# Block attention into a mixture of experts: another order of first loads and constants, later value sums, and routing in three batches

## The chip, the cores and the metric

One core of one Trainium2 chip runs the kernel. The metric is the device time of one execution in microseconds (us). The engines are PE (TensorE), DVE (VectorE), ACT (ScalarE), POOL (GpSimd) and SP (SyncE, which here issues DMAs); PEld is the weight load of PE.

## The reference, cut to what matters

First the attention, for 4 batches, 8 heads, 768 positions and 64 columns. Each query sees the keys within 15 positions on either side, and one summary of each of the 24 blocks of 32 keys: the maximum of the keys and the mean of the values. Then a mixture of experts on the 3072 rows of 512 columns that come out: 4 groups of 4 experts, of which each row goes to one.

```
k_sum = k.reshape(B, H, nb, block, D).max(axis=3)
v_sum = v.reshape(B, H, nb, block, D).mean(axis=3)
mask_l = np.abs(pos[:, None] - pos[None, :]) < window
scores_s = scale * np.einsum('bhsd,bhnd->bhsn', q, k_sum) + np.log(block)
scores_all = np.concatenate([np.where(mask_l, scores_l, -1e9), scores_s], axis=-1)
a = softmax(scores_all)
x = np.matmul(a, np.concatenate([v, v_sum], axis=2))   # then as (3072, 512)
g_idx = argmax(x @ w_group);  e_idx = argmax(x @ w_expert[g_idx])
w = softmax(group logits)[g_idx] * softmax(expert logits)[e_idx]
out[tok] = w * (relu(x[tok] @ w1[g, e]) @ w2[g, e])    # w1 512x1024, w2 1024x512
```

## The kernel before

**Attention.** The work goes by pairs of heads: `idx` = 0 to 15, and each pair has three steps of four tiles of 64 queries, so a step is `n` = 3 idx + g, from 0 to 47. `PLAN` (L46) sets what a step does and in which order: scores of step n (`scores`, L724: PE into `ps_s`, DVE's `ss` with the row maximum `nm`, then ACT's `pr` in `exps`), the transposes of the step before (`transpose_p`), the products with the values of the step before that (`values`), and pieces of the preparation of the next pair (`prep`, L685). Of a pair, `load_qk` (L559) loads `qn` and `kn` (128x768 each), `repack` (L668) copies them into `qr` and `kr`, `prep` transposes them on PE into `ktp` and `qbd`, reduces the key maxima `ks` and builds `kw`. `load_vw` (L573) loads the value windows `va` of a pair, in four DMAs (two of 96x10x64 and two of 80x2x64), into a ring of four; `init_va` (L612) sets the parts that no DMA writes. `load_vn` (L586) loads the values of four heads, 96x2048; `v_summaries` (L645) halves them on POOL five times, and a sixth operation makes the means `vs`. `put_vs` (L655) moves the means of a pair to the right partitions by two DMAs (`vr`), which SP issues, and POOL spreads `vr` over `va` with `pool_copy` (L1211, a multiplication by one). The table `VN` (L55) says at which pair a batch's half is loaded (third number) and summed (fourth).

**Order.** The program runs each engine's instructions in the order in which the code issues them; nothing is reordered. An engine waits at an instruction until its inputs are there, and everything behind it waits too. The DMAs that SP issues are such a row as well. Before the loop stands the start-up sequence (L814 to L833).

**Routing.** `Router.consts` (L164) makes constants by IOTA on POOL, some of which DVE finishes (`lower`, `ones`, `seen`). `Router.route` (L227) takes a batch of columns of 128 tokens (24 in all): maxima, one-hot rows (`goh`, `eoh`), then `ranks` (L265) with matmuls of `eb` by `tri` and `ones`, from which come each token's place and its one-hot row `ohr`, and the weights `w_all`. It is a generator that the attention's loop and later the experts' loop drive a step at a time, through a first-in, first-out list `work`. The first 12 columns are routed from step 28 on, then `first_blocks` picks the rows of the first four experts' blocks; the last 12 (`fin`, L1251) run after the attention. `slots` (L372) makes the table of the tokens of a block: it compares (`eq`), multiplies with three columns, the token number on POOL and the two halves of the weight on DVE (`bo`), and multiplies on PE with `ohr`. From the result come `gather`, `weight` and `scatter`. `unit_slots` (L503) does so for the units, whose columns it takes from three look-ups.

**Experts.** `Experts` (L895) multiplies in two parts: ACT casts a weight to `w1h` or `w2h`, and a subtraction gives the rest, `w1l` or `w2l` (`split_w`, L969); the activations are split alike (`hTh`, `hTl`, `xT`). `first` (L1136) works the first four blocks, `rest` (L1159) the pairs of units. `hook` (L1221) places the first weights' loads, gathers and splits at steps near the end of the attention; `W1_COPY` and `W1_POOL` move parts of the split of w1 to POOL. `gather` (L983) reads rows of x by an indirect DMA from POOL; `y` is the product of an output with its weight.

Of the kernel before, what the change touches and what calls it, by code (L numbers as in the profile page):

```python
# [20 lines left out]
P = 128  # L21
# [42 lines left out]
SPLIT_AT = (-4, -3, 1, 2)  # L64
W1_COPY, W1_POOL = (0,), (0, 1)
# [70 lines left out]
class Router:  # L136
# [235 lines left out]
    def slots(self, name, col, nt, step, c0):  # L372
# [4 lines left out]
        for j0 in range(0, nt, step):  # L377
            js = slice(j0, j0 + step)
            bo = self.tmp.tile([P, step, 3, n], F32R, name="bo_" + name, bufs=2)
            eq = self.tmp.tile([P, step, n], F32, name="eq_" + name, bufs=2)  # L380
            V.tensor_tensor(out=eq, in0=iob.broadcast_to([P, step, n]), in1=bc(col[:, js], n), op=ALU.is_equal)
            yield
            nc.gpsimd.tensor_tensor(out=bo[:, :, 0], in0=eq, in1=bc(self.tok1[:, js], n), op=ALU.mult)
            for i in range(2):
                V.tensor_tensor(out=bo[:, :, 1 + i], in0=eq, in1=bc(self.w[:, js, i].bitcast(F32), n), op=ALU.mult)
                yield
            yield from self.pause(SLOT_AHEAD)
            if j0 == 0:
                sl = self.ps["tr" if nt == step else "lg"].next()[:, 0:3 * n].rearrange("p (a s) -> p a s", a=3)
            for j in range(step):  # L390
                jj = j0 + j
                self.T.matmul(out=sl.rearrange("p a s -> p (a s)"), lhsT=self.ohr[:, jj],
                                 rhs=bo[:, j].rearrange("p a s -> p (a s)"), start=(jj == 0), stop=(jj == nt - 1))
# [127 lines left out]
def attention(tc, q, k, v, w_group, w_expert, ident, pool_copy, x_dram, ps, router, hook):  # L521
# [24 lines left out]
    with ExitStack() as st, ExitStack() as nat_st:  # L546
# [284 lines left out]
        for t in prr:  # L831
            V.memset(t[:, :, NC:NR], 1.0)
# [469 lines left out]
```

## Time and profile before

| what | before |
|---|---|
| time, median of 3 runs | 594.27 us (593.92 to 594.61) |
| time of the profiled execution | 593.2 us |
| its span, first to last instruction | 591.5 us |
| mean granted clock of PE | 0.951 of full |
| busy PE, DVE, ACT, POOL | 527.7, 361.9, 289.3, 207.7 us |
| PE busy share in 40 slices, tenths | 5369899898989796897999999999999999999992 |
| DMA busy share in 40 slices, tenths | 9939699998634452049965566667765665538600 |

A slice is 14.8 us. PE is busy 89% of the span; its low digits stand in the first three slices, in the 16th and 17th (222 to 251 us) and in the last. The time beside the span (593.2 less 591.5) is 1.7 us.

### The profile page before, as it was taken

Reading aid. Unit: us, or ns where it says so; the run is one execution under the profiler, and the core shown is the slowest. Engines: PE = TensorE matmul, PEld = TensorE weight load, DVE = VectorE, ACT = ScalarE, POOL = GpSimd, SP = SyncE. Lnnn points to the kernel's source line nnn. Section 1 sums busy time; section 2 is a strip of 40 time slices with the busy share of each in tenths; the row PEclk is TensorE's granted clock in tenths of the full one; section 3 lists DMA queues with packets and bytes.
Section 4 is the critical chain, followed back from the end, with each engine's and each line's share of the span. In section 5 each row is a group of like instructions: output and inputs, shape, how many; then the busy total and the mean of one; then the engine's idle time right before and its main releaser. Section 6 shows DMA issues by size and latency. Waiting matters only on the chain.

```text
span 591.5 us, 11036 instructions
## 1 busy us (share of the span) xinstructions
PE 527.7 (89%) x4004; PEld 452.9 (77%) x4004; DVE 361.9 (61%) x928; ACT 289.3 (49%) x552; POOL 207.7 (35%) x195
## 2 busy tenths in 40 slices
PE   5369899898989796897999999999999999999992
PEld 2357777686868685795989989899899898877770
DVE  6279999879998478694747465474474564700000
ACT  3247687686768365011646355464464464611110
POOL 6274728755964535126202212123023021211110
PEclk8669999898989798799999999999999999999997
DMA  9939699998634452049965566667765665538600
GB/s 203 199 60 234 152 224 199 256 180 228 150 56 142 149 200 87 12 169 394 373 245 205 201 224 237 232 196 240 254 204 189 241 220 224 187 95 327 258 20 21
DMA packets 95192, 113.63 MB, mean 192 GB/s; under 512 B 43742, under 2 KB 68366, under 8 KB 90512
## 3 DMA queue, kind: packets, MB, share of 16 engines
q1 hardware_dynamic: 89008, 95.41, 56.3%
q0 software_dynamic: 4960, 15.21, 6.9%
q10 hardware_dynamic: 1152, 2.12, 1.1%
q8 instruction: 36, 0.59, 0.4%
q14 instruction: 36, 0.29, 0.2%
HBM read 108.31 MB, written 13.63 MB: 206 GB/s over the span
## 4 chain that ended last, share of the span: by engine, by line
PE 33%; DMA 22%; issue 21%; DVE 17%; POOL 3%; SPq 2%; ACT 1%; POOLq 0%; DVEq 0%; ACTq 0%
DMA out_dram<-y,t_unit_scatter 17%; PE ps_av L121 12%; PE ps_s L121 12%; PE ps_tr L121 8%; DVE qr L675 3%; DVE ss L736 2%; DMA qn<-in_q_dram 2%; DVE kw L722 2%; DVE kw L717 2%; DMA xd<-x_dram,t_unit_gather 2%; DVE ks L682 1%; DMA x_dram<-xt 1%; DVE kr L673 1%; DVE xt L767 1%; POOL va L1211 1%
## 5 line engine op out<-in xcount | busy, mean ns | idle before, releaser
L1025 POOL DMA_INDIRECT out_dram<-y,t_unit_scatter x24 | 26.0, 1085 | 230.1 <-ACT y L1018 114.0
L121 DVE TENSOR_TENSOR w2l<-w2r,w2h 128x1024 fp32r<-128x1024 f32 x40 | 49.1, 1226 | 68.4 <-ACT w2h L980 68.4
L121 PE MATMUL ps_s<-xT,w1h 128*128 128x256 f32 x448 | 84.0, 285 | 0.0
L744 ACT ACTIVATE pr<-ss,nm 128x120 f32<-128x120 f32 x192 | 60.2, 386 | 42.7 <-DVE nm L736 42.2
L121 PE MATMUL ps_av<-w2h,hTh 128*128 128x512 f32 x192 | 76.8, 400 | 0.0
L121 PE MATMUL ps_av<-w2l,hTh 128*128 128x512 f32 x192 | 76.5, 398 | 0.0
L121 PE MATMUL ps_av<-w2h,hTl 128*128 128x512 f32 x192 | 76.5, 398 | 0.0
L121 PEld LDWEIGHTS ps_s<-xT,w1h 128*128 128x128 f32 x448 | 71.0, 192 | 0.6 <-issue 0.3
L121 PE MATMUL ps_tr<-ident,pr 128*121 128x128 f32 x192 | 41.5, 322 | 25.4 <-ACT pr L744 25.1
L121 PE MATMUL ps_s<-xT,w1l 128*128 128x256 f32 x224 | 63.4, 283 | 0.0
L1063 ACT ACTIVATE hTh<-ps_s 128x512 fp32r<-128x512 f32 x48 | 28.7, 597 | 70.4 <-PE ps_s L121 50.0
L121 PE MATMUL ps_s<-kw,qbd 128*128 128x120 f32 x384 | 59.8, 303 | 2.2 <-DVE kw L722 1.5
L1211 POOL TENSOR_TENSOR va<-vr,one 24x1536 f32<-24x1536 f32 x16 | 45.2, 2822 | 45.1 <-DMA vr<-vs 32.3
L121 PEld LDWEIGHTS ps_tr<-ident,pr 128*121 128x121 f32 x192 | 29.6, 192 | 37.6 <-ACT pr L744 32.3
L121 PE MATMUL ps_s<-ohr,w1h 128*128 128x256 f32 x320 | 57.8, 280 | 0.0
L121 PEld LDWEIGHTS ps_s<-kw,qbd 128*128 128x128 f32 x384 | 50.9, 207 | 5.8 <-ACT qbd L698 1.7
L121 DVE TENSOR_TENSOR w1l<-w1r,w1h 128x1024 fp32r<-128x1024 f32 x44 | 51.0, 1221 | 2.7 <-ACT w1h L980 2.7
L121 PEld LDWEIGHTS ps_s<-ohr,w1h 128*128 128x128 f32 x320 | 49.4, 188 | 0.2
L121 DVE SCALAR_TENSOR_TENSOR hTl<-ps_s,hTh 128x512 fp32r<-128x512 f32 x48 | 33.2, 691 | 24.5 <-ACT hTh L1063 24.5
L980 ACT CAST w2h<-w2r 128x1024 fp32r<-128x1024 f32 x44 | 45.6, 1040 | 1.4 <-DMA x_dram<-xt 1.2
L121 PE MATMUL ps_s<-ohr,w1l 128*128 128x256 f32 x160 | 44.5, 278 | 0.0
L651 POOL TENSOR_TENSOR vn_w<-vn_w 96x1024 f32<-96x1024 f32 (+4 forms) x40 | 42.3, 1058 | 5.7 <-DMA vn_w<-in_v_dram 3.1
(216 smaller groups left out, 1037.6 us busy)
## 6 DMA issues: line engine op xcount, KB each, us to landing
w1r<-in_moe_w_dram SPq DMA_DIRECT2D x32, 1024.0 KB
w2r<-in_moe_w_dram SPq DMA_DIRECT2D x32, 1024.0 KB
va<-in_v_dram SPq DMA_DIRECT2D x32, 240.0 KB
kn<-in_k_dram SPq DMA_DIRECT2D x16, 384.0 KB
qn<-in_q_dram SPq DMA_DIRECT2D x16, 384.0 KB
vn_w<-in_v_dram SPq DMA_DIRECT2D x8, 768.0 KB
x_dram<-xt SPq DMA_DIRECT2D x12, 512.0 KB
vn_w<-in_moe_w_dram SPq DMA_DIRECT2D x2, 1024.0 KB
```

Source lines behind the costliest of these rows:

```text
L121: return f(*args, **kw)
L651: nc.gpsimd.tensor_tensor(out=a[:, 0:w], in0=a[:, 0:w], in1=a[:, w:2 * w], op=ALU.add)
L673: copy(out=kr.rearrange("p c j h d -> p (c j) h d"), in_=kn.rearrange("p h c j d -> p (c j) h d"))
L675: copy(out=qr[:, :, :, h], in_=qn[:, h].rearrange("p c j d -> p j c d"))
L717: V.tensor_copy(out=kw[:, :, 0:KW], in_=win)
L722: (pool_copy if idx in POOL_KS else V.tensor_copy)(out=kw[:, :, KW:NC], in_=ks[:, None, :].broadcast_to([P, NQT, NBLK]))
L736: V.tensor_tensor_reduce(out=ss[:, i], in0=mask[:, 1 if t == 0 else 2 if t == NQT - 1 else 0], in1=sp[:, i], scale=1.0, scalar=3.4e38, op0 ...
L744: nc.scalar.activation(out=pr[:, i, 0:NC], in_=sp[:, i], func=AF.Exp, bias=nm[:, i:i + 1], scale=-1.0)
L980: (copy or self.nc.scalar.copy)(out=h, in_=src)
L1025: self.nc.gpsimd.indirect_dma_start(out=self.out, out_offset=bass.IndirectOffsetOnAxis(ap=self.tabs[name, "scatter"][:, col:col + 1], axis=0),
L1063: nc.scalar.activation(out=th[:, js], in_=hp, func=AF.Relu)
L1211: tc.nc.gpsimd.tensor_tensor(out=out, in0=in_, in1=by, op=ALU.mult)
```

## The change

It does six things. (1) The start-up: `va` of pair 0 is loaded ahead of q and k of pair 1, `va` of pair 1 ahead of q and k of pair 2; the second half of the values, the router's weights and q and k of pair 3 come behind them. The routing's constants are made in the start-up and no longer at the end of step 0. The first value sum is one reduction and a scaling on DVE. The `vr` DMAs of pairs 0 and 1 are issued by POOL, and `put_vs` is cut in two (`put_vs`, `spread_vs`). `repack` of pair 1 stands in step 0 behind its scores, and the second sum in step 1. (2) `VN` has the sums two pairs behind their loads. (3) The routing has a third batch of columns, 12 to 17, put on the work list at step 40; after the attention only 18 to 23 are left, and tiles are named by the batch's size. (4) `slots` goes over its groups twice, first with the token column, then with the two weight columns, and signals the gather table ahead of the weights; all products are DVE's. (5) `unit_slots` looks up one value into which three are packed, and takes it apart by integer operations. (6) The splits of w1 of the first blocks are all ACT's and DVE's, at the attention's last four steps, the subtraction for their w2 is DVE's, and `y` is ACT's everywhere.

```
-VN = ((1, 0, 1, 2), (1, 1, 2, 3), (2, 0, 3, 5), (2, 1, 4, 6), (3, 0, 6, 8), (3, 1, 9, 10))
+VN = ((1, 0, 1, 2), (1, 1, 2, 4), (2, 0, 4, 6), (2, 1, 6, 8), (3, 0, 8, 10), (3, 1, 9, 11))
-SPLIT_AT = (-4, -3, 1, 2)
-W1_COPY, W1_POOL = (0,), (0, 1)
+SPLIT_AT = (-4, -3, -2, -1)
...
         qk = {0: load_qk(0)}
         load_vn(0, vn_t, 0)
-        qk[1] = load_qk(1)
...
+        init_va(0)
+        load_vw(0)
+        qk[1] = load_qk(1)
...
-        def v_summaries(b, g):
+        def v_summaries(b, g, vector=False):
...
+            if vector:
+                V.reduce_sum(out=vss[b][:, g], in_=a.rearrange("q k d -> q d k"), axis=AX.X)
+                V.tensor_single_scalar(vss[b][:, g], vss[b][:, g], 1.0 / BLOCK, op=ALU.mult)
+                return
...
-        def put_vs(idx):
+        def put_vs(idx, queue=None):
...
-                nc.sync.dma_start(out=vr[KW:NC, 0, h], in_=vs[h4 * NBLK:(h4 + 1) * NBLK, g])
+                (queue or nc.sync).dma_start(out=vr[KW:NC, 0, h], in_=vs[h4 * NBLK:(h4 + 1) * NBLK, g])
+            vrs[idx] = vr
+
+        def spread_vs(idx):
+            vr = vrs.pop(idx)
             pool_copy(out=va_ring[idx % NVA][KW:NC, :, :, 0:D], in_=vr[KW:NC].broadcast_to([NBLK, NQT, 2, D]))
...
-        init_va(0)
-        load_vw(0)
-        qk[2] = load_qk(2)
         repack(0)
...
-        v_summaries(0, 0)
-        put_vs(0)
-        load_vn(0, vn_t, 1)
-        qk[3] = load_qk(3)
+        for t in prr:
+            V.memset(t[:, :, NC:NR], 1.0)
+        v_summaries(0, 0, True)
+        router.consts()
+        for i in range(2):
+            put_vs(i, nc.gpsimd)
+        spread_vs(0)
         init_va(1)
         load_vw(1)
-        put_vs(1)
-        for t in prr:
-            V.memset(t[:, :, NC:NR], 1.0)
-        repack(1)
+        qk[2] = load_qk(2)
+        spread_vs(1)
+        load_vn(0, vn_t, 1)
...
+        qk[3] = load_qk(3)
...
                     sps = scores(n)
+                    if n == 0:
+                        repack(1)
...
-                router.consts()
+            if n == 1:
                 v_summaries(0, 1)
...
+            if n == ROUTE_2_AT:
+                work.append(router.route(2 * TB, 3 * TB))
...
+        def columns(values):
+
+            for j0, eq in zip(groups, eqs):
+                js = slice(j0, j0 + step)
+                bo = self.tmp.tile([P, step, 2, n], F32R, name="bo_" + name, bufs=2)[:, :, 0:len(values)]
+                if values[0] is self.tok1:
+                    V.tensor_tensor(out=eq, in0=iob.broadcast_to([P, step, n]), in1=bc(col[:, js], n), op=ALU.is_equal)
+                    yield
+                for i, v in enumerate(values):
+                    V.tensor_tensor(out=bo[:, :, i], in0=eq, in1=bc(v[:, js], n), op=ALU.mult)
+                    yield
+                yield from self.pause(SLOT_AHEAD)
...
+                    self.T.matmul(out=sl, lhsT=self.ohr[:, jj], rhs=bo[:, j].rearrange("p a s -> p (a s)"),
+                                  start=(jj == 0), stop=(jj == nt - 1))
+            return sl
+        sl = yield from columns([self.tok1])
...
         self.ready |= 2
...
+        ws = yield from columns([self.w[:, :, i].bitcast(F32) for i in range(2)])
+        self.ready |= 4
...
-        lk = []
-        for i in range(3):
-            lk.append((yield from self.look_up(self.ut[:, i], NT, f"ulook{i}")))
+
+        base = 2 * NPAIR + 2
+        lk = yield from self.look_up(self.ut, NT, "ulook")
...
-        if self.fixed:
-            self.nc.scalar.activation(out=y, in_=yp, func=AF.Copy, scale=w)
-        else:
-            self.V.tensor_scalar_mul(y, yp, w)
+        self.nc.scalar.activation(out=y, in_=yp, func=AF.Copy, scale=w)
...
-                    self.split_w(("first", 0), 1, [k - 4], sub=self.nc.gpsimd)
+                    self.split_w(("first", 0), 1, [k - 4])
...
-                ex.split_w(("first", 0), 0, [part], pool_copy if part in W1_COPY else None,
-                               tc.nc.gpsimd if part in W1_POOL else None)
+                ex.split_w(("first", 0), 0, [part])
...
-        fin = chain(router.route(2 * TB, NT), two(router.unit_slots, router.unit_rows))
+        fin = chain(router.route(3 * TB, NT), two(router.unit_slots, router.unit_rows))
...
             ex.gather2(0)
+            yield
+
+            while not router.ready & 4:
+                yield
             ex.gather2(1)
```

On SP, the first rows of the program before, from the first load on; `kn` and `qn` are keys and queries, `va_110` and `va_111` the value windows of pairs 0 and 1, `vn` the values to be summed, `vr` the put of the means:

```order
L564 DMA kn<-in_k_dram 128x6x128
L564 DMA qn<-in_q_dram 128x6x128
L587 DMA vn_w_116<-in_v_dram 96x2048
L564 DMA kn<-in_k_dram 128x6x128
L564 DMA qn<-in_q_dram 128x6x128
L582 DMA va_110<-in_v_dram 96x10x64 x2
L583 DMA va_110<-in_v_dram 80x2x64
L584 DMA va_110<-in_v_dram 80x2x64
L564 DMA kn<-in_k_dram 128x6x128
L564 DMA qn<-in_q_dram 128x6x128
L662 DMA vr<-vs 24x64 x2
L587 DMA vn_w_116<-in_v_dram 96x2048
```

And the same place of SP's program after the change:

```order
L586 DMA kn<-in_k_dram 128x6x128
L586 DMA qn<-in_q_dram 128x6x128
L609 DMA vn_w_116<-in_v_dram 96x2048
L604 DMA va_110<-in_v_dram 96x10x64 x2
L605 DMA va_110<-in_v_dram 80x2x64
L606 DMA va_110<-in_v_dram 80x2x64
L586 DMA kn<-in_k_dram 128x6x128
L586 DMA qn<-in_q_dram 128x6x128
L604 DMA va_111<-in_v_dram 96x10x64 x2
L605 DMA va_111<-in_v_dram 80x2x64
L606 DMA va_111<-in_v_dram 80x2x64
L586 DMA kn<-in_k_dram 128x6x128
```

Both `va` loads moved ahead of a pair's `kn` and `qn`, and no `vr` stands among these loads any more.

On POOL, the program before, behind the last start-up memsets; `inv` is a constant, the rows of L651 halve the values, L1211 is the copy into `va`, the IOTAs are the routing's constants:

```order
L637 MEMSET inv 96x64
L651 TENSOR_TENSOR vn_w_116<-vn_w_116 96x1024
L651 TENSOR_TENSOR vn_w_116<-vn_w_116 96x512
L651 TENSOR_TENSOR vn_w_116<-vn_w_116 96x256
L651 TENSOR_TENSOR vn_w_116<-vn_w_116 96x128
L651 TENSOR_TENSOR vn_w_116<-vn_w_116 96x64
L653 TENSOR_TENSOR vs<-vn_w_116,inv 96x64
L1211 TENSOR_TENSOR va_110<-vr,one 24x24x64
L1211 TENSOR_TENSOR va_111<-vr,one 24x24x64
L169 IOTA iom_307 128x4
L169 IOTA io_309 128x128
L169 IOTA tok_311 128x24
```

After the change POOL has this from the same memset on:

```order
L661 MEMSET inv 96x64
L167 IOTA iom_237 128x4
L167 IOTA io_239 128x128
L167 IOTA tok_241 128x24
L167 IOTA row 32x1
L167 IOTA lower 128x256
L179 AFFINE_SELECT tri<-ones 128x128
L167 IOTA ioe 128x16
L167 IOTA io_254 32x16
L690 DMA vr<-vs 24x64 x4
L1246 TENSOR_TENSOR va_110<-vr,one 24x24x64
L1246 TENSOR_TENSOR va_111<-vr,one 24x24x64
```

The constants moved ahead of both copies into `va`, the first sum's six rows left POOL, and four `vr` DMAs came to it.

On DVE, the program before at the end of the attention; `hTl` belongs to the first blocks, `tl` and `lg` are the last logits, and the others are the routing of columns 12 to 23 (128x240 is 12 columns):

```order
L804 STREAM_TRANSPOSE tl<-lT 128x192
L805 COPY lg<-tl 128x120
L121 SCALAR_TENSOR_TENSOR hTl_2627<-ps_s_67,hTh_2626 128x512
L121 TENSOR_REDUCE mx_2917<-lg 128x60
L121 TENSOR_TENSOR dd<-lg,mx_2917 128x240
L121 SCALAR_TENSOR_TENSOR c_2921<-dd,iom_307 128x240
L121 TENSOR_REDUCE mx_2917<-c_2921 128x60
L121 TENSOR_TENSOR c_2921<-iom_307,mx_2917 128x240
L121 TENSOR_TENSOR eoh<-c_2921 128x192
L121 CAST sb<-seen 128x16
L121 SCALAR_TENSOR_TENSOR hTl_2627<-ps_s_66,hTh_2626 128x512
```

After the change, around the same `tl` and `lg`; the routing here is that of columns 12 to 17, and between the two pieces stand 14 more rows of it:

```order
L119 SCALAR_TENSOR_TENSOR hTl_2621<-ps_s_66,hTh_2620 128x512
L836 STREAM_TRANSPOSE tl<-lT 128x192
L837 COPY lg<-tl 128x120
L119 TENSOR_TENSOR c_6_2825<-iom_237,mx_6_2806 128x120
L119 TENSOR_TENSOR eoh<-c_6_2825 128x96
L119 CAST sb_2902<-seen 128x16
L119 TENSOR_REDUCE cs_2904<-eoh 128x16
L119 CAST eb_2906<-eoh 128x96
...
L119 TENSOR_TENSOR w_all<-wf_2935,w_all 128x6
L119 SCALAR_TENSOR_TENSOR hTl_2621<-ps_s_67,hTh_2620 128x512
L119 TENSOR_TENSOR w2l_2951<-w2r_2614,w2h_2950 128x1024 x2
L119 SCALAR_TENSOR_TENSOR hTl_2621<-ps_s_66,hTh_2620 128x512
```

A whole batch of routing came between the first and the second `hTl`, and the four `w2l` that were POOL's came between the ones that follow; the last batch stands behind them.

## Rows read from the trace of the kernel before

**Rows 1.** Windows: stretch, length, busy us (and count) per engine, granted clock, DMA share, GB/s

```profile
20.00:34.00 14.00, 0.00 (x0) 0.00 (x0) 0.66 (x6) 0.15 (x1) 6.36 (x8) 0.57 0.97 180
...
224.00:246.00 22.00, 14.99 (x98) 13.60 (x97) 16.53 (x27) 7.09 (x11) 9.59 (x4) 0.77 0.05 18
246.00:286.00 40.00, 35.93 (x220) 31.57 (x219) 29.90 (x88) 7.87 (x11) 14.12 (x13) 1.00 0.69 263
286.00:520.00 234.00, 234.00 (x1516) 212.38 (x1515) 135.63 (x141) 123.11 (x160) 44.23 (x40) 1.00 0.65 224
```

**Rows 2.** Timeline of start-up: start, duration, instruction, idle before and releaser

```profile
10.09 5.59 POOL L651 TENSOR_TENSOR vn_w<-vn_w 96x1024 f32<-96x1024 f32 x5 [3.05 <-DMA vn_w<-in_v_dram]
...
11.68 1.16 DVE L673 COPY kr<-kn 128x768 f32<-128x768 f32 x1 [1.58 <-DMA kn<-in_k_dram]
...
17.04 0.94 DVE L682 TENSOR_REDUCE ks<-ktp 128x24 f32<-128x768 f32 x1
...
26.24 1.53 SPq L662 DMA_DIRECT2D vr<-vs  x2
...
29.61 2.74 POOL L1211 TENSOR_TENSOR va<-vr,one 24x1536 f32<-24x1536 f32 x1 [7.03 <-DMA vr<-vs]
...
33.34 0.29 DVE L121 TENSOR_SCALAR lower<-lower 128x256 f32<-128x256 f32 x1 [13.97 <-POOL lower L169]
...
33.71 0.26 DVE L736 CUSTOM_DVE_ANT_0 ss<-mask,ps_s 128x120 f32<-128x120 f32 x1
...
34.46 1.43 PE L121 MATMUL ps_tr<-ident,pr 128*121 128x128 f32 x4 [14.70 <-ACT pr L744]
...
36.99 2.22 DVE L675 COPY qr<-qn 128x384 f32<-128x384 f32 x2
```

**Rows 3.** Timeline, pair 3's copies, and a just-in-time sum, its load, its repack

```profile
48.07 0.62 DVE L675 COPY qr<-qn 128x384 f32<-128x384 f32 x2
...
62.67 0.32 POOL L653 TENSOR_TENSOR vs<-vn_w,inv 96x64 f32<-96x64 f32 x1
...
64.66 0.45 SPq L564 DMA_DIRECT2D kn<-in_k_dram  x1
...
83.05 0.55 DVE L673 COPY kr<-kn 128x768 f32<-128x768 f32 x1
```

**Rows 4.** Timeline of the first blocks' slots and splits, and one earlier copy

```profile
43.13 3.03 POOL L1211 TENSOR_TENSOR va<-vr,one 24x1536 f32<-24x1536 f32 x1 [2.75 <-DMA vr<-vs]
...
198.68 0.67 POOL L1211 TENSOR_TENSOR kw<-ks,one 128x288 f32<-128x288 f32 x1
198.77 2.21 PE L121 MATMUL ps_tr<-bo_first,ohr 128*128 128x12 f32 x12 [3.80 <-POOL bo_first L383]
...
206.23 2.17 DVE L121 TENSOR_TENSOR t_first_weight<-sc 128x4 f32<-128x4 f32 x1
...
211.11 2.16 DVE L121 TENSOR_TENSOR hi<-hi,lo 128x4 int32<-128x4 int32 x1
...
218.75 1.22 DVE L121 TENSOR_TENSOR w1l<-vn_w,w1h 128x1024 fp32r<-128x1024 f32 x1
```

**Rows 5.** Timeline of the late routing

```profile
228.40 9.59 POOL L981 TENSOR_TENSOR w2l<-w2r,w2h 128x1024 fp32r<-128x1024 f32 x4 [10.34 <-ACT w2h L980]
...
228.98 2.10 DVE L121 TENSOR_TENSOR c<-iom,mx 128x240 f32<-128x240 f32 x1
...
238.16 0.34 PE L121 MATMUL ps_tr<-eb,tri 128*128 128x192 bf16 x1 [7.01 <-DVE eb L121]
```

**Rows 6.** Timeline of a look-up, the units' slots and their gathers

```profile
252.71 0.55 DVE L121 TENSOR_TENSOR look<-eoh,ut 128x384 f32<-128x384 f32 x1
...
262.29 0.80 PE L121 MATMUL ps_lg<-bo_unit,ohr 128*128 128x162 f32 x6
...
268.27 0.87 PE L121 MATMUL ps_lg<-bo_unit,ohr 128*128 128x162 f32 x6 [1.00 <-DVE bo_unit L121]
...
277.77 0.75 PE L121 MATMUL ps_tr<-ident,xd 128*128 128x128 f32 x4 [1.58 <-DMA xd<-x_dram,t_unit_gather]
```

More of the change, by code (lines that the diff above doesn't have):

```diff
@@ L261, in route, with ranks @@
         yield
-        ranks = self.ranks(j0, j1, dd, goh, eb, sb)
+        ranks = self.ranks(j0, j1, tl, dd, goh, eb, sb)
         yield from both(self.units(), ranks) if j1 == NT else ranks
-    def ranks(self, j0, j1, dd, goh, eb, sb):
+    def ranks(self, j0, j1, tl, dd, goh, eb, sb):
         nc, V = self.nc, self.V
-        n, js, tl = j1 - j0, slice(j0, j1), self.tile
+        n, js = j1 - j0, slice(j0, j1)
         nc.scalar.activation(out=dd, in_=dd, func=AF.Exp)
@@ L376, in slots @@
         iob = self.io128[:, :, c0:c0 + n]
[L377 to L393, printed above, removed]
@@ L395, in slots @@
-        V.tensor_scalar(out=t[name, "gather"], in0=sl[:, 0], scalar1=-1.0, scalar2=0.0, op0=ALU.add, op1=ALU.max)
-        sc = self.tile("sc", 3, n)
-        V.tensor_copy(out=sc, in_=sl)
+        groups = range(0, nt, step)
+        eqs = [self.tile("eq_%s%d" % (name, j0), step, n) for j0 in groups]
+        def columns(values):
[9 more added lines that the diff above has]
+                yield from self.pause(SLOT_AHEAD)
+                if j0 == 0:
+                    sl = self.ps["tr" if nt == step else "lg"].next()[:, 0:len(values) * n]
+                for j in range(step):
+                    jj = j0 + j
+                    self.T.matmul(out=sl, lhsT=self.ohr[:, jj], rhs=bo[:, j].rearrange("p a s -> p (a s)"),
+                                  start=(jj == 0), stop=(jj == nt - 1))
+            return sl
@@ L458, in units @@
         yield
+        for i in (1, 2):
+            V.scalar_tensor_tensor(out=ut[:, 0], in0=ut[:, i], scalar=64.0 ** i, in1=ut[:, 0], op0=ALU.mult, op1=ALU.add)
+            yield
+        self.ut = ut[:, 0]
     def unit_rows(self):
@@ L855, in attention @@
                 init_va(3)
-                router.consts()
+            if n == 1:
                 v_summaries(0, 1)
-                nc.gpsimd.memset(wcat[:, :, 20:32], 0.0)
-                nc.sync.dma_start(out=wcat[:, :, 0:4], in_=w_group.rearrange("(a p) g -> p a g", p=P))
-                for i in range(G):
-                    nc.sync.dma_start(out=wcat[:, :, 4 + 4 * i:8 + 4 * i], in_=w_expert[i].rearrange("(a p) e -> p a e", p=P))
             if n == ROUTE_AT:
```

45 lines of the change are left out of this document (33 added, 12 removed).

## The prediction, made before the changed kernel ran

> **What bounds the kernel now.** I first read the table of windows, cut where the kind of work changes, and compared in each the time PE is busy with the length of the window [rows 1]. From 286 to 520 us PE is busy all 234.00 us: what happens on the other engines there is worth nothing. The stages before it differ. From 20 to 34 us PE runs no instruction at all, DVE six, POOL eight, and the DMA share is 0.97. From 224 to 246 us PE is busy 14.99 of 22 us at a mean granted clock of 0.77, with the DMA queues nearly empty (0.05). From 246 to 286 us it lacks 4 us of 40. So what the change can bring is bounded by a few gaps ahead of 286 us, and I read these in the timeline, always from the PE row with a wait back to its releaser.
>
> *Start-up* [rows 2]. PE's wait of 14.70 us ends at 34.46 by `pr`, which needs `ss` of the second step, at 33.71. DVE stands from 19.4 on at `lower`, a constant of the routing that waits 13.97 us for POOL. POOL has that IOTA behind its copy of the value sums into `va` of pair 1 (29.61 to 32.35), and that copy waits 7.03 us for `vr`, whose DMA SP issues only at 26.24, behind the loads of va1. No number of the attention is missing at 20 us; an order in three queues holds DVE.
>
> *First blocks' slots* [rows 4]: PE waits 3.80 us for `bo_first`, a product on POOL behind another `va` copy. Afterwards DVE operations on 4 columns take 2.17 and 2.16 us.
>
> *Late routing* [rows 5]: PE waits 7.01 us for `eb`. It is the end of a row of DVE operations of which `c` takes 2.10 us, in the shadow of four POOL subtractions (9.59 us together).
>
> *Unit gathers* [rows 6]: 1.00 us for the last `bo_unit`, and twice about 1.5 us for a gathered tile.
>
> **The change, part by part.**
>
> *First loads and constants.* The constants move ahead of the `va` copies on POOL, so `lower` no longer waits for `vr`. What is late next is the loads: DVE's program now has repack(1) ahead of ss of the second step, so kn1 and qn1 decide, and these now stand behind va0. vn0 is there at 10.09 in before [rows 2], and nothing ahead of it moves. Then, at the 180 GB/s of the full queues [rows 1], va0 (0.57 MB) takes 3, kn1 and qn1 (0.39 MB each) 2 each: I take 13.0, 15.0, 16.9. On DVE the first value sum, a reduction over 2048 columns, now stands ahead of the rest: `ks` reduces 768 columns in 0.94 us [rows 2], so 2048 take about 2.3 us, done at 12.4, in the time in which DVE waits for kn1. Then kr1 1.16 us (to 16.2), qr1 about 2.0 (16.9 to 18.9), four small operations of pair 1's preparation about 3.0 with `ks` as the largest, memsets 0.8: ss of the second step at 22.7, 11.0 us before its 33.71. The next step repeats it: qn2 at about 23.7, repack(2) done at 25.2, where before it ended at 39.2. Something is given back: the second value sum, five POOL operations, is now taken some way into the loop, when vn1 lands (about 28), and DVE copies beside it cost more, 2.22 us for `qr` [rows 2] against 0.62 with POOL idle [rows 3], and kr likewise: 2.5 to 3 us, as before, where it lay at 34 to 39. Since before pays the same, I leave **11.0 us**. Bounds: 6 if the transfers that stand behind va0 and va1 land 5 us later than so, 14.5 if the whole gap closes.
>
> *Value loads ahead of the sums.* At four places the sum now ends just before SP's put of it. The row of such a place in before: POOL ends `vs` at 62.99, SP then issues `vr` and, behind it, kn at 64.66; that pair is repacked at 83.05 [rows 3], 18.4 us later, of which the transfer needs 4 or so. I take **0**: a delay of some us of SP there is hidden by this lead; bounds +2 and −2.
>
> *Slots of the first blocks.* The token product goes to DVE and no longer waits for POOL's `va` copy: 3.80 saved [rows 4]. What is late next is `kw`, also behind that copy, at 198.68 [rows 4], about when PE comes to its scores. The subtractions of the split (w1l) leave POOL, so `t_first_weight` (2.17) and `hi` (2.16) fall to about 0.2 each, and a third like them: 5.3 us of DVE, which holds the softmax between; I count 4.5. To pay: 12 more matmuls of about 0.13 us (1.6) and w1l on DVE, 1.22 us each [rows 4]; of four, two were on DVE before, late; I count 1.2. Sum **5.5 us**. Bounds 2 (only the wait, less the costs) and 8.
>
> One rule speaks against the last part. The row: POOL's `va` copy takes 3.03 us at 43.13 beside a busy DVE [rows 4], 2.74 at 29.61 beside an idle one [rows 2]: 0.3 us longer, no block. The Trainium skill, page "SBUF — State Buffer", section "SBUF: two separate sides", says that an operation of VectorE with two SBUF inputs and one of GpSimd that reads SBUF exclude each other for the whole instruction. By that rule each w1l on DVE could hold the POOL copies of `kw` and `va` for 1.22 us, 4.9 in all in place of 1.2, and the sum of this part would be 1.8; the 2.17 us rows agree with it in the other direction. I keep the row's price, since the copies have lead over their use.
>
> *Routing's third batch earlier, w2 split on DVE.* The late routing shrinks from 12 columns of tokens to 6, and w2l leaves POOL, so the wait of 7.01 [rows 5] goes, and with it the low clock behind it: a mean of 0.77 over 22 us [rows 1] is 10 us at 1.2 in place of 2.4 GHz; I put 6 of them into the wait itself and 4 behind it, where PE worked at half speed and lost 2.0. In its place: the third batch's `eb` stands behind hTl(0) and six operations of 0.1 to 0.4 us, while PE has only 12 matmuls before the ranks: a wait of 1.9. hTl(1) then stands behind 22 operations of the same batch, about 4 us with two `ohr` of 384 columns at 0.55 each (the row of `look`, as wide [rows 6]), against 24 matmuls (2.9 us) and 0.8 of ranks with the chain's start: 2.4. The last batch's `eb` stands behind four w2l of 1.22 and three hTl: 2.1 more. So 9.0 saved, 6.4 paid.
>
> *Token column first, one look-up.* Gathers start before the weights are made: I expect the 1.00 and both 1.5 us waits to go (4.1 with their parts) [rows 6]; two look-ups, 0.55 us and a reduction as wide each [rows 6], less on DVE, six small operations more. To pay: 24 more matmuls, by six in 0.80 us [rows 6] 3.2 us. `y` on ACT: off DVE, onto an engine that is busy 7.87 of the 40 us [rows 1]: 0.
>
> Late stage together: 9.0 + 4.1 − 6.4 − 3.2 = **3.5 us**, bounds 0 and 7.
>
> Sum: 11.0 + 5.5 + 3.5 = 20.0 us. The profiled execution took 593.2 us (591.5 of it the span), so 573.2; the median of the runs is 1.07 above that execution, so **574.3**.
>
> **Rivals.**
> - *Paced by transfers.* In 20 to 34 us the queues are 0.97 busy [rows 1] and the same bytes are still to come. If kn2 and qn2 land 5 to 6 us later than I put them, DVE waits there: start-up gains 4.5, the time is about 580.5. Against it: SP could not even issue those loads early in before. 0.13.
> - *Late waits replaced.* The w2l and the 22 routing operations on DVE hold hTl so that nothing of the 3.5 is left: about 578. For it: DVE's program has no slack between those blocks, and four w2l of 1.22 us stand among them. 0.14.
> - *POOL's own DMAs held.* The four `vr` issues now stand on POOL beside DVE's copies of pair 1 at 15 to 19 us; if each waits for the copy that runs, the second `va` copy ends 3 us later and the third step waits: about 577. 0.06. The Trainium skill (the same page and section, the box on the trap of DMAs from GpSimd) states such a mechanism; before has no DMA of this kind beside such copies that would show it.
> - *All waits vanish*, clock at full from 224 on: 14.5 + 8 + 7, about 564. 0.05.
> - *Slower.* SP stands at the puts of sums that are now made just in time, and the loads of q and k queue behind it, at four pairs. The lead is 18.4 less the transfer's 4 [rows 3]. The rest decides: SP must be held over 14 us at a pair before repack waits. Four such, each 6 us beyond it, eat the 20 and 4 more: about 598. For it, the sum's chain (load, 6 us on POOL, put) has no spare step now. 0.04.
> - *No effect*, since another queue holds DVE to 33 us: 594. 0.03.
>
> **How the numbers follow.** The sum as worked out has 0.55, with its own range 569 to 580. The rivals between 577 and 580.5 have 0.33. I give 565 to 585: it leaves out the fastest, the slower, the one with no effect, and the tails. About 0.2%, some 1.2 us, is what a measurement here can tell from no change: faster 0.93, same 0.03, slower 0.04.
>
> **What would show it.** Right: no PE gap over 5 us from 20 to 34; `lower` before 14 us on DVE; ss of the second step near 22.7; PE's first pair of experts starting some 20 us earlier than 285; no wait of 7 us for `eb` but three near 2; DVE's slot operations at 0.2. Wrong: kr2 or qr2 waiting for a DMA past 28 (transfers paced), SP's waits for `vs` growing past 14 us at a pair with `kr` waiting for kn, or PE waiting long for hTl behind routing.

## The result, and the profile after

The changed kernel takes 584.75 us in the median of 4 runs (583.74 to 587.43), the kernel before 594.1 us (593.5 to 594.61). The ratio is 0.9863, with a 95% interval of 0.9829 to 0.9896: faster by 8 to 9 us, where 20 were forecast. The median lies 0.25 us inside the upper end of the range of 565 to 585, and outside the sum's own range of 569 to 580. The profiled execution took 585.12 us, 583.4 of it the span.

The windows of the changed kernel, with the columns of [rows 1]:

```profile
20.00:34.00 14.00, 11.61 (x101) 9.71 (x101) 13.14 (x49) 9.30 (x24) 10.48 (x9) 0.88 0.85 164
47.00:196.00 149.00, 126.03 (x1334) 107.62 (x1329) 114.61 (x472) 100.98 (x261) 93.53 (x75) 0.91 0.77 174
...
224.00:246.00 22.00, 18.92 (x116) 16.13 (x115) 19.40 (x71) 7.52 (x11) 1.74 (x2) 1.00 0.04 13
246.00:286.00 40.00, 37.34 (x268) 34.71 (x267) 23.95 (x60) 14.35 (x20) 12.45 (x11) 1.00 0.93 347
286.00:520.00 234.00, 233.25 (x1510) 211.13 (x1509) 129.93 (x135) 119.86 (x156) 43.61 (x39) 1.00 0.60 210
```

The empty stretch from 20 to 34 us is full, and the clock of 224 to 246 us is at its upper level throughout. But the long middle, from 47 to 196 us, has PE busy for only 126 of 149 us, fewer than in the kernel before, whose row of that stretch is

```profile
47.00:196.00 149.00, 134.65 (x1440) 112.05 (x1440) 137.01 (x530) 110.74 (x287) 89.68 (x73) 0.97 0.83 186
```

The forecast had put the effect on this stretch at nothing.

The start-up, in the timeline of the changed kernel (the pieces that answer to [rows 2]):

```profile
9.61 3.59 DVE L674 TENSOR_REDUCE vs<-vn_w 96x64 f32<-96x2048 f32 x1
...
13.35 0.28 DVE L119 TENSOR_SCALAR lower<-lower 128x256 f32<-128x256 f32 x1
...
15.00 0.55 DVE L705 COPY kr<-kn 128x768 f32<-128x768 f32 x1
...
19.11 5.51 POOL L1246 TENSOR_TENSOR va<-vr,one 24x1536 f32<-24x1536 f32 x2 [2.43 <-DMA vr<-vs]
...
22.97 0.25 DVE L768 CUSTOM_DVE_ANT_0 ss<-mask,ps_s 128x120 f32<-128x120 f32 x1
...
23.71 1.23 PE L119 MATMUL ps_tr<-ident,pr 128*121 128x128 f32 x4 [2.22 <-ACT pr L776]
```

`lower` runs at 13.35, `kr` of pair 1 at 15.00, `ss` of the second step at 22.97 (forecast 22.7). PE's wait of 14.70 us, before, is now one of 2.22.

To see where the lead went, I took from each timeline the start of `ss` of some steps (counted from 0, so the second step is step 1), and two later points: the first matmul of the first blocks, and the last gathered tile's transposes (`ps_tr<-ident,xg`) before the units. All in us from the start of the span:

| point | before | changed | lead |
|---|---|---|---|
| step 2 | 39.13 | 27.69 | 11.4 |
| step 17 (end of pair 5) | 96.01 | 76.93 | 19.1 |
| step 18 (pair 6) | 97.69 | 85.09 | 12.6 |
| step 28 | 135.13 | 123.55 | 11.6 |
| step 43 | 193.10 | 189.81 | 3.3 |
| first blocks | 218.09 | 214.64 | 3.5 |
| gathered tile | 284.80 | 276.01 | 8.8 |
| end | 591.5 | 583.4 | 8.1 |

The start-up's lead grows to 19 us and 16 of it are gone by step 43. Between step 43 and the first blocks, where the slots lie, nothing is added on balance (3.3 to 3.5); the late stage brings 5.3.

What PE and SP waited for, in the views of waits of the changed kernel (waiter, releaser: us in total, times, longest):

```profile
PE ps_s L119 <- POOL kw L1246: 14.8, 4, 6.2
...
SPq L690 <- POOL vs L681: 36.1, 6, 8.5
```

And the longest of PE's four waits, at pair 6, in the timeline:

```profile
70.04 5.89 POOL L679 TENSOR_TENSOR vn_w<-vn_w 96x1024 f32<-96x1024 f32 x5
...
72.93 0.94 DVE L714 TENSOR_REDUCE ks<-ktp 128x24 f32<-128x768 f32 x1
...
76.00 0.52 POOL L681 TENSOR_TENSOR vs<-vn_w,inv 96x64 f32<-96x64 f32 x1
76.55 1.54 SPq L690 DMA_DIRECT2D vr<-vs  x2
...
79.34 2.74 POOL L1246 TENSOR_TENSOR va<-vr,one 24x1536 f32<-24x1536 f32 x1 [2.82 <-DMA vr<-vs]
...
82.17 0.67 POOL L1246 TENSOR_TENSOR kw<-ks,one 128x288 f32<-128x288 f32 x1
...
82.89 2.06 PE L119 MATMUL ps_s<-kw,qbd 128*128 128x120 f32 x8 [6.17 <-POOL kw L1246]
```

The reader is to see one chain in POOL's program: the sum (70.04 to 76.5), its own put through SP and the DMA queues, on which the spread into `va` waits 2.82 us, and only behind that spread the small copy into `kw`, for which `ks` was ready at 73.9. Pair 6 is the first whose `kw` POOL copies (`POOL_KS`). PE stands for 6.17 us for a copy of 0.67, and its scores then run at the lower of its two clocks, 1.2 GHz: 2.06 us for eight at a granted clock of 0.50, where eight took 1.15 us at 1.00 before the wait (at 72.78).

The slots and the late stage of the changed kernel, beside [rows 4 to 6]:

```profile
190.04 1.47 PE L119 MATMUL ps_tr<-bo_first,ohr 128*128 128x4 f32 x12 [1.50 <-DVE bo_first L119]
...
202.18 0.16 DVE L119 TENSOR_TENSOR t_first_weight<-sc_first 128x4 f32<-128x4 f32 x1
...
203.78 1.23 DVE L119 TENSOR_TENSOR w1l<-vn_w,w1h 128x1024 fp32r<-128x1024 f32 x1 [1.01 <-ACT w1h L1018]
...
209.28 1.24 PE L119 MATMUL ps_tr<-ident,xg 128*128 128x128 f32 x8 [1.42 <-ACT xT L820]
...
211.35 0.67 PE L119 MATMUL ps_tr<-ident,pr 128*121 128x128 f32 x4 [0.84 <-ACT pr L776]
...
227.15 0.38 PE L119 MATMUL ps_s<-xT,w1h 128*128 128x256 f32 x1 [1.45 <-DVE hTl L119]
...
237.08 0.20 PE L119 MATMUL ps_tr<-eb,tri 128*128 128x96 bf16 x1 [1.63 <-DVE eb L119]
...
276.01 0.72 PE L119 MATMUL ps_tr<-ident,xg 128*128 128x128 f32 x4 [2.38 <-DMA xg<-x_dram,t_unit_gather]
```

The forecast's repairs are there: `t_first_weight` at 0.16, `eb` no longer waited for 7 us, the replaced waits at 1.45 and 1.63. At the slots a wait of 1.50 for DVE's `bo_first` stands in place of 3.80 for POOL's, and at the gathers one of 2.38. New are the short waits from 209 us on, behind ACT and DVE.

### The profile page after: what moved, and what is told of

Same layout as the page of the kernel before. It is cut to its first block, busy times and chain, and to the rows that moved or that the text cites. A ratio compares the mean times of both kernels' runs of the same rounds, so it can differ in the third digit from the quotient of the medians.

```text
span 583.4 us, 11124 instructions
## 1 busy us (share of the span) xinstructions
PE 526.4 (90%) x4041; PEld 454.4 (78%) x4041; DVE 346.8 (59%) x964; ACT 293.2 (50%) x558; POOL 186.0 (32%) x181
## 4 chain that ended last, share of the span: by engine, by line
PE 44%; issue 20%; DMA 13%; DVE 12%; POOL 6%; ACT 2%; SPq 0%; ACTq 0%; POOLq 0%; DVEq 0%
PE ps_s L119 19%; PE ps_av L119 15%; DMA out_dram<-y,t_unit_scatter 9%; PE ps_tr L119 9%; POOL va L1246 2%; DVE ss L768 2%; DVE kw L749 1%; DMA xg<-x_dram,t_unit_gather 1%; DVE ks L714 1%; POOL vn_w L679 1%; DMA vr<-vs 1%; DVE qr L707 1%; DMA qn<-in_q_dram 1%; ACT pr L776 1%; PE ps_lg L119 1%
## 5 line engine op out<-in xcount | busy, mean ns | idle before, releaser
L119 DVE TENSOR_TENSOR w2l<-w2r,w2h 128x1024 fp32r<-128x1024 f32 x44 | 53.8, 1226 | 72.3 <-ACT w2h L1018 71.8
L119 PE MATMUL ps_av<-w2h,hTh 128*128 128x512 f32 x192 | 76.5, 398 | 0.0
L119 PE MATMUL ps_s<-kw,qbd 128*128 128x120 f32 x384 | 61.4, 309 | 16.5 <-POOL kw L1246 14.8
L119 PEld LDWEIGHTS ps_s<-kw,qbd 128*128 128x128 f32 x384 | 52.3, 211 | 20.3 <-POOL kw L1246 15.4
L1246 POOL TENSOR_TENSOR va<-vr,one 24x1536 f32<-24x1536 f32 x16 | 44.5, 2782 | 61.5 <-DMA vr<-vs 44.8
L768 DVE CUSTOM_DVE_ANT_0 ss<-mask,ps_s 128x120 f32<-128x120 f32 x192 | 41.7, 271 | 15.3 <-PE ps_s L119 15.1
L119 PE MATMUL ps_tr<-ident,pr 128*121 128x128 f32 x192 | 39.0, 314 | 6.4 <-ACT pr L776 6.3
L1055 ACT ACTIVATE y<-ps_av,t_unit_weight 128x512 f32<-128x512 f32 x20 | 13.8, 688 | 61.8 <-PE ps_av L119 44.1
```

Of the source, the lines that this page charges most:

```text
L119: return f(*args, **kw)
L768: V.tensor_tensor_reduce(out=ss[:, i], in0=mask[:, 1 if t == 0 else 2 if t == NQT - 1 else 0], in1=sp[:, i], scale=1.0, scalar=3.4e38, op0 ...
L1055: self.nc.scalar.activation(out=y, in_=yp, func=AF.Copy, scale=w)
L1246: tc.nc.gpsimd.tensor_tensor(out=out, in0=in_, in1=by, op=ALU.mult)
```

## The experiments

Ratios are to the kernel before in runs on the same chip; 0.001 is 0.6 us. "Lead" is, as above, by how much a step starts earlier than in the kernel before. It is read from one profiled execution of each kernel.

**The table of sums, two ways.** e1 is the changed kernel with the old table, e2 the kernel before with the new one.

```
-VN = ((1, 0, 1, 2), (1, 1, 2, 4), (2, 0, 4, 6), (2, 1, 6, 8), (3, 0, 8, 10), (3, 1, 9, 11))
+VN = ((1, 0, 1, 2), (1, 1, 2, 3), (2, 0, 3, 5), (2, 1, 4, 6), (3, 0, 6, 8), (3, 1, 9, 10))   # e1; e2 the other way
```

> The changed kernel with the table VN of before (sums one or two pairs earlier), all else as changed. Theory A (POOL's program: a sum made just in time holds the spread into va, and the key summaries kw of a pair stand behind that spread, so PE waits for kw 14.8 us in four places): these four waits shrink to under 3 us in all, and the time falls from 584.75 by 12 to 16, to 569 to 573. Rival B (the sums slow DVE's copies wherever they stand, and the lead is lost to that): the number of sums is the same, so 583 to 587. Rival C (the third routing batch on DVE takes the lead): 583 to 587, with the PE waits for kw still small.

> The kernel before with the new table VN alone. Theory A: the same waits of PE for kw appear in it, 8 to 15 us in all, and the time is 602 to 609, slower than 594.1. Its SP is later from the start than in the changed kernel, so it may be at the upper end. Rivals B and C: 593 to 596.

Measured: e1 0.9804 (0.9743 to 0.9865), 581.44 us; e2 1.0078 (1.0051 to 1.0105). The new table costs 3.5 us beside the start-up and 4.6 alone; the first figure is not clear of noise by itself (the intervals of e1 and of the changed kernel overlap), the second is. That is theory A's sign with a quarter (e1) to a half (e2) of its size: PE's waits for `kw` were 6.7 us in e1 and 8.8 in e2. In e1 the lead falls at one place, from 18.8 us at step 17 to 9.5 at step 20, and then stays between 9.3 and 10.4 to step 43. There the wait has the same shape without any sum ahead of it:

```profile
73.65 1.55 SPq L690 DMA_DIRECT2D vr<-vs  x2
...
80.58 2.74 POOL L1246 TENSOR_TENSOR va<-vr,one 24x1536 f32<-24x1536 f32 x1 [7.69 <-DMA vr<-vs]
...
84.12 2.06 PE L119 MATMUL ps_s<-kw,qbd 128*128 128x120 f32 x8 [6.04 <-POOL kw L1246]
```

(Timeline of e1.) The put is issued at 73.65, behind loads of `va`, and POOL gets it at 80.58. The steps behind show what the table does: from step 36 to 43 the changed kernel's lead falls from 9.2 to 3.3, past a wait for `kw` of 4.30 us, and e1's, which has the same routing and differs in the table alone, goes from 9.4 to 9.5.

**kw out of the spread's shadow, two ways.** e3 moves the spread one step later on POOL; e4 makes the copy into `kw` on DVE.

```
-                    spread_vs(idx + 2)                       # e3: out of step 2 of a pair ...
+            if g == 0 and 0 < idx < len(order) - 1:          # ... into the next step, behind kw
+                spread_vs(idx + 1)
-POOL_KS, ACT_K1 = range(6, B * NP), range(10, B * NP)        # e4
+POOL_KS, ACT_K1 = (), range(10, B * NP)
```

> The changed kernel with the new table VN, in which only the spread into va of a pair is moved one step later on POOL, behind the next kw; va of that pair is first read five steps later. Theory A: kw no longer stands behind a copy that waits for vr, PE's waits for kw fall from 14.8 to under 4 us, the time is 569 to 575. Rivals B and C: 583 to 587.

> The changed kernel with the copy of the key summaries into kw on DVE for all pairs (ten copies of 0.3 us move from POOL). Theory A: PE no longer waits for POOL's kw, 14.8 us go, about 3 us of DVE work come: 571 to 577. Rivals B and C: 585 to 590.

Measured: e3 0.9843 (0.9797 to 0.989), e4 0.981 (0.9764 to 0.9856). The wait at pair 6 goes (lead 18.6 and 18.8 us at step 18), and yet e3 is no faster than the changed kernel. The view of waits of e3 shows who waits in its place:

```profile
PE ps_tr L119 <- POOL kr L1247: 13.1, 5, 4.5
...
PE ps_s L119 <- POOL kw L1247: 4.3, 2, 2.6
```

For pairs 10 and 12 to 15 POOL also copies `kr` and `qr` (`POOL_QK`), and these stand behind the same spreads. Theory A as I had put it, with `kw` alone, falls. e4, with an interval that overlaps the changed kernel's, shows the same: PE waits 10.8 us for POOL's `kr`.

**Is it the transfers?** e5 has POOL issue all puts; e8 drops the loads of the values to be summed from the loop.

```
-                    put_vs(idx + 2)
+                    put_vs(idx + 2, nc.gpsimd)               # e5
-                    if idx == at:
-                        load_vn(b1, vn_t, g1)                # e8
```

> The changed kernel with all vr DMAs issued by POOL instead of SP, so that SP never waits for a sum and POOL issues vr right behind it. Theory A2 (POOL's and SP's programs hold each other: POOL's sum, then SP's put, then POOL's spread, with SP's loads queued behind the put): the lead of the start-up is kept longer, 572 to 578. Theory D (the transfers themselves pace the attention from 60 to 130 us, a small vr lands only after the large loads ahead of it): 582 to 587, vr landing no sooner.

> The changed kernel without the six loads of values to be summed inside the loop (5 MB in all); the sums are still made, from what stands in the tile, so the block means of batches 1 to 3 are not those of the reference. Theory D: the queues have room, vr lands sooner, SP's loads too, the lead is kept: 568 to 575. Theory A2: the sums, puts and spreads stay in their order, so 580 to 585.

Measured: e5 1.0279 (1.0211 to 1.0347), slower than before by 14 (medians) to 17 us (ratio). Neither theory had that. e8's block means change its routing, and with it the number of units, so its whole time (540.16 us) says nothing; its attention can be read. There the lead at step 18 is 15.3 us (12.6 with the loads) and at step 43 7.0 (3.3): without these loads some 3 to 4 us more of it are kept, not 16. At pair 6 itself PE doesn't wait for `kw` in e8 (its only such wait is 3.5 us, later): the sum that began at 70.04 begins at 64.48. But POOL's waits for `vr` are 44.3 us in all, as in the changed kernel (44.8). The loads of q, k and `va` stay in e8, so what those take is not shown. In e5 (its timeline, and the view of the tile `vr`):

```profile
89.76 2.74 POOL L1246 TENSOR_TENSOR va<-vr,one 24x1536 f32<-24x1536 f32 x1 [5.99 <-DMA vr<-vs]
...
93.30 1.00 PE L119 MATMUL ps_s<-kw,qbd 128*128 128x120 f32 x3 [16.26 <-POOL kw L1246]
...
DMA to landing us min/median/max: 1.5/4.3/8.7
```

A put is two DMAs of 6 KB; from POOL each lands 4.3 us after its issue in the median and up to 8.7. From SP a put took 2.8 us from the issue to its use in the changed kernel (76.55 to 79.34) and 6.9 in e1, so another issuing engine does not get it past the large loads. And every put, also of a pair without a new sum, now waits its turn in POOL's own program, where SP had issued it ahead. The Trainium skill, page "DMA: Bandwidth & Descriptors", section "Issuing engines are not separate DMA queues", says that DMAs from any engine run on the same 16 DMA engines and interleave there; by that rule e5's puts gain only the time of issue, and the trace agrees: POOL's waits for `vr` are 43.1 us in all.

**All copies that PE needs off POOL.** e6 is the changed kernel so, e9 the same with the old table, e16 the kernel before so.

```
-POOL_QK = (10, 12, 13, 14, 15)
-POOL_KS, ACT_K1 = range(6, B * NP), range(10, B * NP)
+POOL_QK = ()
+POOL_KS, ACT_K1 = (), range(10, B * NP)
```

> The changed kernel with the copies into kw, kr and qr on DVE for every pair, so that no copy that PE waits for stands on POOL behind a spread. Theory A2: the lead of about 20 us that stood at pair 6 without kw's wait is kept to the end of the attention, less about 6 us of DVE work: 570 to 576. Theory D: the lead is lost to some load that lands late, PE or DVE then waits for a DMA or for va, 579 to 585.

> The changed kernel with both edits that helped: the table VN of before, and the copies into kw, kr and qr on DVE for every pair. Theory E (POOL's program is late at a sum by 6 us of its own plus its put's transfer, and PE takes the loss wherever a copy that it needs stands behind; the sums two pairs later only make POOL later): the lead of 19 us at pair 5 passes pair 6 and is kept, less about 5 us of DVE work: 568 to 574, faster than with the DVE copies alone (577.5). Rival F (DVE is the bound once the copies are on it, the table no longer matters): 575 to 580.

> The kernel before with the copies into kw, kr and qr on DVE alone. If these copies on POOL cost only where the start-up's lead runs into them: no gain here, 593 to 597, ratio 0.999 to 1.006. If they cost in any order: 585 to 590, ratio 0.985 to 0.993.

Measured: e6 0.9694 (0.9608 to 0.9779), e9 0.9738 (0.9707 to 0.9769), e16 0.9989 (0.9954 to 1.0024). Alone the edit gives nothing; on top of the start-up it gives more (e6 10 us by the ratios below the changed kernel; e9 4 below e1, with intervals that overlap), and e6 and e9 cannot be told apart, so the table shows no effect any more. In e6 the lead is 17.1 us at step 18 and 20 at step 36. It falls to 11.6 by step 40, now with DVE's routing operations as what PE waits for (e6's timeline):

```profile
158.69 0.17 PE L119 MATMUL ps_tr<-sbt,ones 128*128 128x16 bf16 x1 [2.49 <-DVE sbt L119]
...
163.55 0.69 PE L119 MATMUL ps_tr<-ident,xt 128*128 128x128 f32 x2 [3.76 <-DVE cnt L119]
```

**The parts alone.** e7 is the kernel before with the start-up part only (its hunks in the diff, from the first loads to `v_summaries(0, 1)`). e10 is the kernel before with the slots in two passes, the one look-up, `y` on ACT and the w1 split on ACT and DVE; e17 the same with the old w1 split; e11 the changed kernel with the old w1 split; e13 the kernel before with the w2 subtraction on DVE; e12 the changed kernel with two routing batches.

```
-                    self.split_w(("first", 0), 1, [k - 4], sub=self.nc.gpsimd)      # e13
+                    self.split_w(("first", 0), 1, [k - 4])
-SPLIT_AT = (-4, -3, -2, -1)                                                         # e11, e17
+SPLIT_AT = (-4, -3, 1, 2)
+W1_COPY, W1_POOL = (0,), (0, 1)
...
-            if n == ROUTE_2_AT:                                                      # e12
-                work.append(router.route(2 * TB, 3 * TB))
-        fin = chain(router.route(3 * TB, NT), two(router.unit_slots, router.unit_rows))
+        fin = chain(router.route(2 * TB, NT), two(router.unit_slots, router.unit_rows))
```

> The kernel before with the start-up part alone: order of first loads, constants, first sum on DVE, first vr DMAs on POOL. If the start-up's lead is not kept (the old VN in the changed kernel showed a lead of 9.4 us from pair 6 on, whatever it was at pair 5): 583 to 587 against 594, a gain of 8 to 10. If the lead of 17 to 19 us at pair 5 is lost only through the later parts of the change: 575 to 579.

> The kernel before with the slots in two passes, one look-up, the w1 split on ACT and DVE and y on ACT; start-up, VN, two routing batches and the w2 subtraction on POOL as before. By the prediction's terms (5.5 us at the first blocks' slots, up to 4.1 at the gathers, less 3.2): 587 to 590. By the steps of the changed kernel's trace (nothing gained between the third-last and the last attention step): 591 to 595, PE's wait of 3.8 us gone and longer steps in its place.

> The kernel before with the slots in two passes, one look-up and y on ACT, but the w1 split as before. If the w1 split's move ate the slots' gain (3.5 to 4 us by the changed kernel with the old split): 588 to 591 against 593.4, ratio 0.992 to 0.996. If the slots alone give nothing: ratio 0.998 to 1.002.

> The changed kernel with the split of the first w1 as before (two parts on POOL, two after the attention). If w1l on DVE and w1h on ACT inside the last four steps ate the gain at the slots: those four steps get shorter by 3 to 5 us, the time 580 to 583. If the two passes of the slots ate it, or POOL's subtractions slow DVE again as before: 584 to 588.

> The kernel before with one edit: the subtractions of the first blocks' w2 on DVE instead of POOL. If these four subtractions of 2.4 us on POOL, beside which the routing's operations took 2 us each, were the late wait: PE's wait of 7 us for eb falls to under 4, the time falls by 3 to 6, ratio 0.990 to 0.995. If the length of the late routing was the wait: no change, ratio 0.998 to 1.002.

> The changed kernel with the routing of columns 12 to 23 in one late batch again, the w2 subtraction staying on DVE. If the third batch is what shortens the late stage by 5 us: 588 to 592, with a PE wait of 4 to 6 us for eb. If it is the w2 subtraction's leaving POOL that ended the 7 us wait: 583 to 587.

Measured: e7 0.9822 (0.9768 to 0.9876), e10 1.0006 (0.9983 to 1.0029), e17 0.9938 (0.9917 to 0.9959), e11 0.9796 (0.9764 to 0.9828), e13 0.9945 (0.992 to 0.9969), e12 0.9855 (0.9827 to 0.9882). In us of 594: the start-up alone −10.6; slots, look-up and `y` −3.7; the w1 split's move +4.0, the same by e10 against e17 and by the changed kernel against e11; the w2 subtraction −3.3; the third batch nothing. With the table's +4.6 the parts come to −9.0, the change measured −8.1 by its ratio, so that the parts add within the noise.

Where the w1 split's 4.0 us go shows in part in e11's timeline: the three short waits of the changed kernel from 209 to 214 us (1.42, 0.84 and 0.82) are not there, and PE comes to the first blocks at 212.50 instead of 214.64, half of the 4.0. Where the other half lies is not shown. Whether the casts on ACT or the subtractions on DVE cost more, no run tells.

Two rows show what each late part leaves. e10 keeps the wait for `eb`; e13 loses it and waits longer at the gathers instead:

```profile
237.07 0.34 PE L119 MATMUL ps_tr<-eb,tri 128*128 128x192 bf16 x1 [7.25 <-DVE eb L119]
```

```profile
271.94 1.13 PE L121 MATMUL ps_tr<-ident,xd 128*128 128x128 f32 x4 [5.75 <-DMA xd<-x_dram,t_unit_gather]
```

The changed kernel, which has both edits, waits 1.63 for `eb`, not at all for `xd`, and 2.38 for the other gathered tile, `xg`.

**Versions faster than both.** e14 is e6 with the old w1 split, e18 is e14 with two routing batches, e15 the kernel before with start-up, e6's copies and the w2 subtraction.

> The changed kernel with the copies into kw, kr and qr on DVE and the split of the first w1 as before. The two gains (about 7 and 3.5 us below the changed kernel) add if they lie in different stages: 573 to 577, ratio 0.964 to 0.970. If the second part of the lead goes to waits at the slots anyway: 578 to 581, ratio 0.973 to 0.978.

> The kernel before with three edits: the start-up part, the copies into kw, kr and qr on DVE, the w2 subtraction on DVE; table, slots, w1 split and two routing batches as before. If these are what counts: 572 to 577, ratio 0.963 to 0.971, as fast as the best version of the changed kernel. If the third batch or the new slots pay only with the lead kept: 578 to 583.

> The fastest version (copies into kw, kr and qr on DVE, old w1 split) with two routing batches instead of three. If the third batch takes DVE time that paces the attention there: its lead of 21 us at pair 11 shrinks less, 571 to 574. If it is worth what it costs, as in the changed kernel: 575 to 578. If the late stage needs it once w2l stands on DVE: 578 to 582.

Measured: e14 0.9679 (0.9623 to 0.9734), 576.06 us; e15 0.9745 (0.9709 to 0.9782), 578.47 us; e18 0.9649 (0.9627 to 0.9671), 572.2 us. e18 is the fastest, 12 to 13 us under the changed kernel, without the third batch. Its interval overlaps e14's, so it is not shown that the third batch costs anything there, only that it isn't needed. Nor does e14 stand clear of e6: with the copies off POOL, a gain from the old w1 split is not shown. e15 falls into its second range, some 6 us behind e18, which has the new slots and the new table as well.

## Why the prediction was wrong, by its own steps

Beside the terms of the sum, what the runs give for the same parts (us gained):

| part | forecast | measured | by |
|---|---|---|---|
| start-up | 11.0 | 10.6 | e7 |
| later sums | 0 | −4.6 | e2 (−3.5 by e1) |
| slots, look-up, `y` | 3.80 − 1.6 + 4.1 − 3.2 = 3.1 | 3.7 | e17 |
| w1 split moved | 4.5 − 1.2 = 3.3 | −4.0 | e10 against e17 |
| w2 subtraction, third batch | 9.0 − 6.4 = 2.6 | 3.3 | e13, e12 |
| sum | 20.0 | 9.0 | changed kernel: 8.1 |

Two steps failed, the later sums and the w1 split; by 4.6 and 7.3 us they make up the 11 us that are missing, the other parts gave 0.9 more than forecast. That 584.75 still lies inside the stated range is luck: the range had been widened for rivals that did not come about.

**Start-up, "I leave 11.0 us": right.** `lower`, POOL's order and the time of `ss` came as described, and e7 gives 10.6. Sizes inside it were off and cancelled, so that 22.97 lies so near 22.7 is partly luck. The first sum took 3.59 us, not 2.3. The loads of pair 1 did not decide: `kr` runs at 15.00 right behind the first step's `ss`, without a wait for a load, and both copies were done at 16.1 (forecast 18.9). Pair 1's preparation then took longer, with `kw` at 2.15 us beside POOL's copy, and `qr` of pair 2 took 2.79 us, so that step 2 began at 27.69. What the forecast did not see is that the lead is not a constant: it grows to 19 us at pair 5, and what arrives at the end is what the first engine that is behind lets through. That was POOL at pair 6.

**"Value loads ahead of the sums: I take 0": the first step that failed.** The place was found, the sum just ahead of its put. But the prediction asked only what stands behind the put on SP, found a lead of 18.4 us there, and priced the delay at nothing. SP's waits did grow, from 7.4 us in all in before to 36.1, the longest 8.5, under the 14 at which the slower rival would decide; no load of q or k was missed. The one that waits was on POOL: spread behind put, and `kw`, `kr`, `qr` behind spread. The price is 3.5 (e1, not clear of noise) to 4.6 us (e2). The right question had stood one paragraph on, for the slots: "What is late next is `kw`, also behind that copy".

**"Sum 5.5 us" at the slots: gone, by the w1 split, the second step that failed.** The gain of the two passes is real, 3.7 us with the look-up and `y` (e17). The w1 split's move was credited with 4.5 us of short DVE operations and priced at 1.2; on balance it costs 4.0. The operations did get short (`t_first_weight` 0.16), but that was not worth its sum to PE, and in e17, with the old split, `t_first_weight` is already at 0.13. The price was taken from a row in which a POOL copy beside a busy DVE grew by 0.3 us. The rule of the Trainium skill weighed there (page "SBUF — State Buffer", section "SBUF: two separate sides"), by which the price would be 4.9 and the sum of the part 1.8, came nearer, but the trace does not show its mechanism: from 196 to 224 us POOL is busy for only 3.93 us in the changed kernel, with four gathers and no copy. PE's short waits stand behind ACT's `xT`, `pr` and `ptS`, into whose row the casts `w1h` had come (1.03 to 1.05 us each), as `w1l` into DVE's (1.22 each); with the old split they are gone (e11). What the prediction left out is the casts on ACT and the place, four steps of the attention in a row.

**"Late stage together 3.5": right in size (5.3 by the points of the table of leads), half right in cause.** The w2 subtraction leaving POOL ends the wait for `eb` (e13); the third batch, with which the prediction's text began, is worth nothing (e12). The waits forecast at 1.9, 2.4 and 2.1 were 0.43, 1.45 and 1.63.

**The rivals.** *Paced by transfers* had 0.13 and a time of 580.5: the time is nearest, but by chance: the start-up did not shrink to 4.5, and neither `kr` nor `qr` waits for a load behind pair 0. e8 shows 3 to 4 us for other loads, in the loop. *POOL's own DMAs held* was put at the start-up, where it cost nothing: `va` of pair 1 ended at 24.62 and the third step did not wait for it. The rest, from 19 us of lead to 3, is by POOL's order (6.7 us of `kw` waits already with the old table, 14.8 with the new one) and, once that is gone, by DVE. DVE's routing is late only for a long lead: through steps 31 to 43 e1 keeps its 9.3 us, while e6, which comes with 19 to 22, goes down to 12. How much of that is the routing alone stays open: no run took the first routing out of the attention.

## What to carry to other kernels

A lead won early is worth only what the slowest engine's program passes on; before booking it at the end, look for the next point at which an engine off the path is already late, here POOL at pair 6. When a producer is moved to just in time, list what stands behind its consumer on every engine that has a piece of the chain, and not only on the queue that issues the transfer: the cheap copy in second place is the one that PE waits for. A repaired wait shows the next one: e13 ends a wait of 7 us and gains 3.3; PE then waits 5.75 at the gathers. And work moved off one engine is to be priced on every engine that gets a piece of it: the w1 split was priced on DVE, and the waits came behind ACT as well.

## What the runs showed of the hardware

- DMAs of 6 KB issued by POOL among large loads landed after 1.5 to 8.7 us, 4.3 in the median (e5). Two of them from SP took 2.8 us from issue to use in the changed kernel (76.55 to 79.34) and 6.9 in e1 (73.65 to 80.58).
- Copies on DVE took two to seven times as long beside POOL's copies and sums as without them (changed kernel): `kw<-ks` 2.15 us at 19.88 against 0.31 at 33.02, `qr` 2.79 for two at 24.97 against 0.62 at 15.47, `kr` 1.30 at 23.75 against 0.55 at 15.00. The reduction `ks` did not: 0.94 us at 72.93 beside a sum on POOL, as without one (0.94 at 32.04).
- A reduction on DVE that reads with a stride of 64 values took 3.59 us for 2048 columns, 1.75 ns each; one over contiguous values 0.95 us for 768, 1.24 ns each (changed kernel; the first is a sum on 96 partitions, the second a maximum on 128).
